# Taking the last two chunks of modes from their sums for the first two pairs of tiles

## The chip, the cores and the metric

The kernel runs on one core of one Trainium2 chip. The metric is the device time of one execution in microseconds (us), lower is better. A timed version is run several times beside the kernel before, on the same chip; the times quoted are medians unless a mean is named. A profile is one execution, so a number from a profile is one draw.

## The reference, cut to what matters

Causal attention of 8 batches x 8 heads x 576 positions feeds a spectral mixing layer:

```python
x = attn_out.transpose(0, 2, 1, 3).reshape(B, S, H * D)      # 8 x 576 x 512
X = np.fft.rfft(x, axis=1)
# 64 modes, each with its own complex 512 x 512 matrix:
Yr = einsum('bmd,mde->bme', Xr, w_r) - einsum('bmd,mde->bme', Xi, w_i)
Yi = einsum('bmd,mde->bme', Xr, w_i) + einsum('bmd,mde->bme', Xi, w_r)
y = np.fft.irfft(Y, n=S, axis=1)
u = x + y
out = u + np.maximum(u @ w_ch, 0.0)
```

The weights `w_r` and `w_i` are 2 x 64 x 512 x 512 f32. Reading them takes most of the time.

## The kernel before: the parts that matter

The 64 modes are taken in 8 chunks of 8. The inverse transform is a matmul with a constant matrix `G` (128 rows: mode, real or imaginary) and with `yv`, which holds y and v = y @ w_ch of all chunks by these 128 rows. A chunk's sums come out as rows of (mode, real or imaginary, batch), so a small transfer from on-chip memory to on-chip memory spreads them over `yv`:

```python
def spread(c, which, rows):
    nc.sync.dma_start(out=yv[16 * c : 16 * c + 16, :, which, :], in_=rows)

def modes(g, c, meanwhile=None):
    ps = auxpool.tile([P, DM], FP32, name="yp", tag="aux")
    for x in range(4):                       # x: one load of weights, 512 KB
        ...
        if x == 3 and meanwhile:
            meanwhile()                      # other matmuls ahead of the last load's
        for cg in range(4):
            nc.tensor.matmul(ps[32 * cg : 32 * cg + 32, :], ...)   # line 441
    ...
            spread(c, 0, yb)                 # last group: y of the chunk

def add_y(dst, i, which, rows=slice(0, P), start=False):   # line 674: from the spread rows
    ... nc.tensor.matmul(dst[x][r, :], G_sb[rows, ...], yv[rows, bb, which, :], ...)

def add_last(dst, i, yb, cols=slice(0, DM)):               # line 683: from a chunk's sums
    ... nc.tensor.matmul(dst[x][:, cols], Gx_sb[:, bass.ts(T, P)], yb[:, cols], ...)
```

`Gx_sb` is `G` of the last chunk, one row in eight, zeros between, so that it picks batch b out of a chunk's unspread sums. The results are made in 18 pairs of tiles. The first two pairs are started while the last weights arrive. The end of the stream of weights, where c is chunk 6 of 0 to 7:

```python
GK = P - 2 * MC                              # 112 rows: chunks 0 to 6
for i in range(NPRE):                        # NPRE = 2 pairs
    x_transposed(i)
x_times_wch(0, False)
yb = modes(NG - 1, c)
yt = y_transposed(yb, c)
y_times_wch(c, yt)                           # v of chunk 6, then spread(c, 1, vb)
x_times_wch(1, False)
start_u(0)
add_y(us[0], 0, 0, slice(0, GK))
def first_sums():
    for i in range(NPRE):
        add_y(z_of(i), i, 1, slice(0, GK))   # needs v of chunk 6 in yv
yb = modes(NG - 1, NCK - 1, first_sums)      # chunk 7
```

The softmax here doesn't subtract the row's maximum and nothing guards it: scores larger than these inputs give would overflow.

Of the kernel before, what the change touches and what calls it, by code (L numbers as in the profile page):

```python
# [9 lines left out]
FP32 = mybir.dt.float32  # L10
FP16 = mybir.dt.float16
# [7 lines left out]
def kernel(  # L19
# [11 lines left out]
    nc = tc.nc  # L31
    B, H, S, D = q.shape
    NM = moe_w_r.shape[0]
    DM = H * D
    P = 128
# [4 lines left out]
    NG = DM // P  # L40
# [5 lines left out]
    MC = 8  # L46
    NCK = NM // MC
# [3 lines left out]
    NF = NT - 1  # L51
# [10 lines left out]
        axis=1,  # L62
# [11 lines left out]
    G_np = np.zeros((NM, 2, SP), dtype=np.float64)  # L74
    G_np[:, 0, :S] = cmv[:, None] * np.cos(ang.T)
    G_np[:, 1, :S] = -(cmv[:, None] * np.sin(ang.T))
    G_np = G_np.reshape(P, SP).astype(np.float16)
# [6 lines left out]
    d_Ff = nc.inline_tensor(Ff_np, name="c_Ffwd").ap()  # L84
    d_G = nc.inline_tensor(G_np, name="c_Ginv").ap()

    Gx_np = np.zeros((2 * MC, B, NF * P), dtype=np.float16)
    Gx_np[:, 0] = G_np[-2 * MC :, : NF * P]
    d_Gx = nc.inline_tensor(Gx_np.reshape(P, NF * P), name="c_Ginvx").ap()

    ctx.enter_context(tc.manual_schedule())
    gp = ctx.enter_context(tc.tile_pool(name="globals", bufs=1))
# [98 lines left out]
    def ring_of(k):  # L191
        if k < NE:
            return None
        return int(k < LW2 and (k - NE) % (WA + WB) >= WA)
# [33 lines left out]
    for n in range(N):  # L228
# [3 lines left out]
        while nt < min(w, len(wq)):  # L232
            i = ring_of(nt)
# [37 lines left out]
    with tc.tile_pool(name="cum_psum", bufs=1, space=PSUM) as cpsum:  # L271
# [5 lines left out]
            out=cum, data0=spos, data1=zer, initial=0.0, op0=ALU.add, op1=ALU.add  # L277
# [16 lines left out]
        for x in range(2):  # L294
            rows = slice(NL * x, NL * x + NL)
            nc.vector.tensor_copy(
                out=cumt4[rows, :], in_=cumt_sb[rows, NK, x::2]
# [132 lines left out]
    def modes(g, c, meanwhile=None):  # L430


        ps = auxpool.tile([P, DM], FP32, name="yp", tag="aux")
        for x in range(4):
            ri, par = divmod(x, 2)
            cols = xs[g % 2].rearrange("p k r b m -> p (k r b) m")
            c0 = (48, 16)[ri] - 16 * par
            if x == 3 and meanwhile:
                meanwhile()
            for cg in range(4):  # L440
                nc.tensor.matmul(  # L441
                    ps[32 * cg : 32 * cg + 32, :],
                    cols[:, c0 : c0 + 32, c * MC + 2 * cg + par],
                    wt[(g, c, ri, par)][:, cg, :],
                    start=(x == 0), stop=(x == 3),
                    tile_position=(0, 32 * cg), skip_group_check=True,
                )
        if g == 0:
            nc.vector.tensor_copy(out=y_acc[:, c, :], in_=ps)
        elif g < NG - 1:  # L450
            nc.vector.tensor_tensor(out=y_acc[:, c, :], in0=ps, in1=y_acc[:, c, :], op=ALU.add)
        else:
            yb = spool.tile([P, DM], FP16, name="y_sb", tag="y")
            for cols in halves if c == NCK - 1 else [slice(0, DM)]:
                nc.vector.tensor_tensor(
                    out=yb[:, cols], in0=ps[:, cols], in1=y_acc[:, c, cols], op=ALU.add
                )
            spread(c, 0, yb)
            return yb
# [3 lines left out]
    def spread(c, which, rows):  # L463

        nc.sync.dma_start(out=yv[16 * c : 16 * c + 16, :, which, :], in_=rows)
# [7 lines left out]
    NPRE = 2  # L473
# [45 lines left out]
    with tc.tile_pool(name="sc_psum", bufs=2, space=PSUM) as scpool, \  # L519
# [7 lines left out]
        for n in range(N):  # L527
# [9 lines left out]
            i = first_pairs[n - N + len(first_pairs)] if n >= N - len(first_pairs) else None  # L537
# [19 lines left out]

    finpool = ctx.enter_context(tc.tile_pool(name="fin_sb", bufs=1))
    yv = finpool.tile([P, B, 2, DM], FP16, name="yv")
    Gx_sb = finpool.tile([P, NF * P], FP16, name="Gx_sb")  # L560
    nc.sync.dma_start(out=Gx_sb, in_=d_Gx)
    upool = ctx.enter_context(tc.tile_pool(name="u_psum", bufs=2, space=PSUM))
    zpool = ctx.enter_context(tc.tile_pool(name="z_psum", bufs=2, space=PSUM))

# [13 lines left out]
    def parts(b, T):  # L578

        if T < NF:  # L580
            return [(slice(0, P), b, ident16h)]
        return [(slice(NL * i, NL * i + NL), b + i, ident16h[:NL, :NL]) for i in range(2)]

    def x_transposed(i):
        xts[i] = xt_sb[len(xts) % 2]
        for x, (b, T) in enumerate(pairs[i]):
            ps = upool.tile([P, DT, P], FP32, name="xt_ps", tag="u")
            for rows, bb, ident in parts(b, T):
                for dt in range(DT):
                    nc.tensor.matmul(  # L590
                        ps[:, dt, rows], x_all[: rows.stop - rows.start, dt, bb, T, :],
                        ident, start=True, stop=True, skip_group_check=True,
                    )
            nc.vector.tensor_copy(out=xts[i][:, x], in_=ps)

    def x_times_wch(i, last):
        zs[i] = z = zpool.tile([P, 2, DM], FP32, name="z_ps", tag="z")
        for x in range(2):
            for dt in range(DT):
                nc.tensor.matmul(  # L600
                    z[:, x, :], xts[i][:, x, dt, :], wch_sb[:, dt, :],
                    start=(dt == 0), stop=(last and dt == DT - 1), skip_group_check=True,
                )
# [16 lines left out]
    def y_transposed(yb, c=NCK):  # L620
        ps = auxpool.tile([P, DT, P], FP16, name="yt_ps", tag="aux")
        for dt in range(DT):
            nc.tensor.transpose(ps[:, dt, :], yb[:, bass.ts(dt, P)], ident16h)
        yt = yt_first[:, :, c, :] if c < NY else spool.tile([P, DT, P], FP16, name="yt_sb", tag="yt")
        nc.scalar.copy(out=yt, in_=ps)
        return yt

    def y_times_wch(c, yt):
        vp = auxpool.tile([P, DM], FP32, name="v_ps", tag="aux")
        for dt in range(DT):  # L630
            nc.tensor.matmul(
                vp, yt[:, dt, :], wch_sb[:, dt, :], start=(dt == 0), stop=(dt == DT - 1)
            )
        vb = spool.tile([P, DM], FP16, name="v_sb", tag="v")
        nc.vector.tensor_copy(out=vb, in_=vp)
        spread(c, 1, vb)
        return vb
# [27 lines left out]
    order_z = list(late)  # L665
    TAKE = (3, 2, 2, 0, 2, 1)
    us, rs = {}, {}
    GK = P - 2 * MC

    def add_y(dst, i, which, rows=slice(0, P), start=False):  # L670

        for x, (b, T) in enumerate(pairs[i]):
            for r, bb, _ in parts(b, T):
                nc.tensor.matmul(  # L674
                    dst[x][r, :], G_sb[rows, bass.ds(T * P, r.stop - r.start)],
                    yv[rows, bb, which, :], start=start, stop=True, skip_group_check=True,
                    tile_position=(0, r.start),
                )

    def add_last(dst, i, yb, cols=slice(0, DM)):  # L680

        for x, (b, T) in enumerate(pairs[i]):
            nc.tensor.matmul(
                dst[x][:, cols], Gx_sb[:, bass.ts(T, P)], yb[:, cols],
                start=False, stop=True, skip_group_check=True,
            )

    def start_u(i):
        pool, tag = ((upool, "u"), (auxpool, "aux"))[i % 2]
        us[i] = [pool.tile([P, DM], FP32, name="u_ps", tag=tag) for x in range(2)]  # L690
        for x, (b, T) in enumerate(pairs[i]):
            for r, bb, ident in parts(b, T):
                nc.tensor.matmul(  # L693
                    us[i][x][r, :].rearrange("p (g d) -> p g d", d=P), ident,
                    x_all[: r.stop - r.start, :, bb, T, :],
                    start=True, stop=False, skip_group_check=True, tile_position=(0, r.start),
                )
# [35 lines left out]
    def z_of(i):  # L733
        return [zs[i][:, x, :] for x in range(2)]

    for c in range(NCK - 2):
        yb = modes(NG - 1, c)
        for x in range(TAKE[c] - 1):
            work()
        yt = y_transposed(yb, c)  # L740
        if TAKE[c]:
            work()
        if c >= NY:
            y_times_wch(c, yt)
        elif c == NY - 1:
            for b in range(B):
                first_times_wch(b)
    work()
    assert not order_z and not ahead
    c = NCK - 2  # L750
    for i in range(NPRE):
        x_transposed(i)
    x_times_wch(0, False)
    yb = modes(NG - 1, c)
    yt = y_transposed(yb, c)
    y_times_wch(c, yt)
    x_times_wch(1, False)


    start_u(0)  # L760
    add_y(us[0], 0, 0, slice(0, GK))

    def first_sums():
        for i in range(NPRE):
            add_y(z_of(i), i, 1, slice(0, GK))

    yb = modes(NG - 1, NCK - 1, first_sums)

    yt = spool.tile([P, DT, P], FP16, name="yt_sb", tag="yt")
    for x in range(2):  # L770
        dts = slice(x * DT // 2, (x + 1) * DT // 2)
        ps = auxpool.tile([P, DT // 2, P], FP16, name="yt_ps", tag="aux")
        for dt in range(dts.start, dts.stop):
            nc.tensor.transpose(ps[:, dt - dts.start, :], yb[:, bass.ts(dt, P)], ident16h)
        nc.scalar.copy(out=yt[:, dts], in_=ps)
    add_last(us[0], 0, yb)
    vb = spool.tile([P, DM], FP16, name="v_sb", tag="v")
    for cols in halves:
# [10 lines left out]
        relu(i, 2 - i)  # L789
    start_u(1)  # L790
    add_y(us[1], 1, 0, slice(0, GK))
    add_last(us[1], 1, yb)


# [65 lines left out]
```

## Time and profile before

| | before |
|---|---|
| three runs known ahead | 460.05, 460.65, 462.11 us |
| the profiled run | 460.51 us, span 458.7 us |
| stream of weights | until about 414 us, then a tail until 418.5 us |
| run of PE matmuls to the end | from about 424 us |

The page's totals of the engines and its row of the granted PE clock (40 slices of 11.5 us, in tenths of full clock) of the kernel before:

```profile
PE 349.6 (76%) x4201; PEld 219.9 (48%) x4201; DVE 236.8 (52%) x527; ACT 219.5 (48%) x382; POOL 182.9 (40%) x269
PEclk9998995999677979966779979799989778988999
```

No engine is near 100% over the span, but each stage has its own limit. The dips in the second line are slices of which a part was granted half clock.

### The profile page before, as it was taken

What the parts mean: (1) busy time and instruction counts of PE and PEld (TensorE: products, weight loads), DVE (VectorE), ACT (ScalarE), POOL (GpSimd) and SP (SyncE); (2) the same over time, 40 slices, a digit from 0 to 9 for tenths busy, and PEclk for the clock granted to TensorE, in tenths of its full rate; (3) what the DMA queues carried; (4) which work ended last, traced back from release to release, by engine and by line L of the source; (5) the groups of instructions that cost most, each with busy time, mean ns of one, the idle gap of its engine ahead of it and who ended that gap; (6) DMA issues with size and microseconds to landing.
All of it is one profiled execution on the core that took longest, in us unless ns stands there. A gap on an engine that the chain in (4) does not pass through costs nothing.

```text
span 458.7 us, 10278 instructions
## 1 busy us (share of the span) xinstructions
PE 349.6 (76%) x4201; PEld 219.9 (48%) x4201; DVE 236.8 (52%) x527; ACT 219.5 (48%) x382; POOL 182.9 (40%) x269
## 2 busy tenths in 40 slices
PE   1879979975663979948497677889977769778995
PEld 1456656753442656624365444556643336434442
DVE  7775654753332646623355444466556416441775
ACT  1586865564242746733356435456612220311895
POOL 6665555544345455344454444455232232100000
PEclk9998995999677979966779979799989778988999
DMA  9999999999999999999999999999999999994688
GB/s 177 201 202 203 201 201 204 202 204 204 205 203 200 202 203 203 204 205 204 198 196 204 204 204 203 204 203 203 205 208 213 210 210 210 214 216 79 237 282 319
DMA packets 109487, 94.63 MB, mean 206 GB/s; under 512 B 28480, under 2 KB 104640, under 8 KB 109440
## 3 DMA queue, kind: packets, MB, share of 16 engines
q0 software_dynamic: 98960, 81.81, 112.6%
q1 hardware_dynamic: 10480, 12.17, 8.5%
q8 instruction: 33, 0.54, 0.4%
q14 instruction: 14, 0.11, 0.1%
HBM read 164.66 MB, written 9.44 MB: 380 GB/s over the span
## 4 chain that ended last, share of the span: by engine, by line
DMA 66%; PE 22%; issue 4%; POOL 3%; DVE 2%; ACT 1%; DVEq 0%; POOLq 0%; ACTq 0%
DMA w_sb<-in_moe_w_i_dram 25%; DMA w_sb<-in_moe_w_r_dram 17%; DMA q<-in_q_dram 13%; DMA k<-in_k_dram 5%; PE sc_ps L365 3%; PE yp L441 3%; DMA x_all<-in_moe_w_r_dram 2%; PE sc_ps L359 2%; DMA y_acc<-in_moe_w_r_dram 2%; PE av_ps L394 2%; PE z_ps L674 2%; PE tr_ps L324 2%; DMA y_acc<-in_moe_w_i_dram 2%; PE u_ps L693 2%; PE u_ps L674 2%
## 5 line engine op out<-in xcount | busy, mean ns | idle before, releaser
L373 ACT ACTIVATE p_sb<-sc_ps,cumt_sb 128x576 f16<-128x576 f32 (+1 forms) x256 | 142.1, 636 | 49.3 <-PE sc_ps L365 48.8
L217 POOL DMA_DIRECT2D w_sb<-in_moe_w_i_dram x60 | 45.1, 751 | 81.6 <-PE yp L441 36.6
L217 POOL DMA_DIRECT2D w_sb<-in_moe_w_r_dram x60 | 45.4, 757 | 65.1 <-DMA w_sb<-in_moe_w_r_dram 28.2
L217 POOL DMA_DIRECT2D v<-in_v_dram x72 | 50.8, 708 | 33.1 <-DMA w_sb<-in_moe_w_r_dram 8.6
L359 PE MATMUL sc_ps<-negm,ident 128*128 128x256 bf16 x256 | 56.3, 306 | 0.2
L324 PE MATMUL tr_ps<-ident,q 64*64 64x64 bf16 x576 | 17.5, 210 | 49.2 <-DMA q<-in_q_dram 49.2
L441 PE MATMUL yp<-w_sb,xs 128*32 128x512 bf16 x480 | 38.0, 419 | 19.0 <-DMA w_sb<-in_moe_w_i_dram 14.7
L327 DVE COPY qtA<-tr_ps 64x576 bf16<-64x576 bf16 x32 | 23.7, 742 | 45.0 <-PE tr_ps L324 45.0
L394 PE MATMUL av_ps<-v,p_sb 128*128 128x65 f16 x1024 | 45.1, 199 | 0.0
L365 PE MATMUL sc_ps<-qtB,ktB 128*128 128x512 bf16 (+2 forms) x192 | 43.6, 344 | 0.0
L344 ACT ACTIVATE p<-sc_ps,cumt 128x64 f16<-128x64 f32 x32 | 10.1, 315 | 69.8 <-PE sc_ps L340 69.8
L394 PEld LDWEIGHTS <-p_sb 128*128 128x128 f16 x1024 | 40.1, 101 | 5.1 <-issue 1.2
L327 DVE COPY ktA<-tr_ps 64x576 bf16<-64x576 bf16 x32 | 24.0, 749 | 32.2 <-PE tr_ps L324 32.2
L324 PEld LDWEIGHTS <-q 64*64 64x64 bf16 x576 | 13.6, 123 | 51.8 <-DMA q<-in_q_dram 51.0
L365 PE MATMUL sc_ps<-qtA,ktA 65*128 65x512 bf16 (+2 forms) x192 | 37.9, 308 | 0.4 <-DMA qtA<-ncum_sb 0.4
L441 PEld LDWEIGHTS <-xs 128*32 128x32 bf16 x512 | 22.8, 170 | 29.8 <-issue 26.5
L399 DVE TENSOR_REDUCE den<-av_ps 128x5 f32<-128x10 f32 x64 | 10.8, 169 | 50.5 <-PE av_ps L394 50.5
L404 DVE TENSOR_TENSOR x_all<-av_ps,rcp 128x320 f16<-128x320 f32 x64 | 31.5, 492 | 2.2
L327 ACT COPY ktB<-tr_ps 64x576 bf16<-64x576 bf16 x32 | 20.3, 636 | 20.8 <-DVE ktA L327 19.9
L324 PE MATMUL tr_ps<-ident,k 64*64 64x64 bf16 x576 | 17.1, 208 | 15.9 <-DVE qtB L327 11.2
L365 PEld LDWEIGHTS <-ktB 128*128 128x128 bf16 x192 | 22.2, 116 | 14.5 <-issue 5.8
L600 PE MATMUL z_ps<-wch_sb,xs 128*128 128x512 f16 x96 | 26.2, 423 | 0.0
(111 smaller groups left out, 530.1 us busy)
## 6 DMA issues: line engine op xcount, KB each, us to landing
w_sb<-in_moe_w_r_dram POOLq DMA_DIRECT2D x60, 512.0 KB, 11.9
w_sb<-in_moe_w_i_dram POOLq DMA_DIRECT2D x60, 512.0 KB, 12.1
q<-in_q_dram POOLq DMA_DIRECT2D x32, 144.0 KB, 10.0
k<-in_k_dram POOLq DMA_DIRECT2D x32, 144.0 KB, 10.1
v<-in_v_dram POOLq DMA_DIRECT2D x72, 64.0 KB, 9.7
out_dram<-r_sb SPq DMA_DIRECT2D x16, 256.0 KB, 2.4
out_dram<-r_w SPq DMA_DIRECT2D x16, 256.0 KB, 2.6
x_all<-in_moe_w_i_dram POOLq DMA_DIRECT2D x3, 512.0 KB, 9.8
```

The costliest lines, as they stand in the source:

```text
L217: nc.gpsimd.dma_start(out=dst, in_=src)
L324: nc.tensor.transpose(ps[rows, r, :], src[rows, r, :], ident16[rows, rows])
L327: copy(out=dst[n % NQ][rows, :].rearrange("d (p r) -> d p r", r=R), in_=ps[rows].rearrange("d r p -> d p r"),)
L359: nc.tensor.matmul(ps[:, bass.ds(w * S, W)], ident16, negm[:, bass.ts(r, W)], start=True, stop=False, skip_group_check=True,)
L365: nc.tensor.matmul(ps[:, c0 : c0 + i1 - i0], keys[:, w, r, :], qt[:, i0:i1], start=False, stop=True, skip_group_check=True,)
L373: nc.scalar.activation(out=pt[:, poff[x] : poff[x] + S - w * W], in_=ps[:, w * S : (w + 1) * S - w * W], func=ACTF.Exp, bias=cumt_sb[:, x, ...
L394: nc.tensor.matmul(ps[:, I, r : r + NCH], lhsT, rhs, start=(i == 0), stop=(i == len(todo) - 1), skip_group_check=True,)
L399: nc.vector.tensor_reduce(out=den, in_=ps[:, :, 0 : VW : NCH], axis=mybir.AxisListType.X, op=ALU.add)
L404: nc.vector.tensor_tensor(out=x_all[:, g, b, :, D * h : D * h + D], in0=ps[:, :, 1 : NCH], in1=rcp.unsqueeze(2).to_broadcast([P, NT, D]), ...
L441: nc.tensor.matmul(ps[32 * cg : 32 * cg + 32, :], cols[:, c0 : c0 + 32, c * MC + 2 * cg + par], wt[(g, c, ri, par)][:, cg, :], start=(x == ...
L600: nc.tensor.matmul(z[:, x, :], xts[i][:, x, dt, :], wch_sb[:, dt, :], start=(dt == 0), stop=(last and dt == DT - 1), skip_group_check=True,)
L674: nc.tensor.matmul(dst[x][r, :], G_sb[rows, bass.ds(T * P, r.stop - r.start)], yv[rows, bb, which, :], start=start, stop=True, skip_group_ ...
```

## The change

Its intent: the z sums of the first two pairs should not wait for the copy of chunk 6's v into `yv`. Both last chunks are taken from their sums, with constants for two chunks. So that these don't double the transfer, only the 16 rows that are not zero are moved, into a cleared tile.

```diff
-    Gx_np = np.zeros((2 * MC, B, NF * P), dtype=np.float16)
-    Gx_np[:, 0] = G_np[-2 * MC :, : NF * P]
+    NX = 2
+    Gx_np = np.stack([G_np[2 * MC * c :, : NF * P][: 2 * MC] for c in range(NCK - NX, NCK)], axis=1)
 ...
-    Gx_sb = finpool.tile([P, NF * P], FP16, name="Gx_sb")
-    nc.sync.dma_start(out=Gx_sb, in_=d_Gx)
+    Gx_sb = finpool.tile([P, NX, NF * P], FP16, name="Gx_sb")
+    nc.vector.memset(Gx_sb.rearrange("p c t -> p (c t)").bitcast(FP32), 0.0)
+    nc.sync.dma_start(out=Gx_sb[0:P:B], in_=d_Gx)
 ...
-    GK = P - 2 * MC
+    GK = P - 2 * MC * NX
 ...
-    for i in range(NPRE):
-        x_transposed(i)
+    x_transposed(0)
     x_times_wch(0, False)
-    yb = modes(NG - 1, c)
-    yt = y_transposed(yb, c)
-    y_times_wch(c, yt)
+    yb6 = modes(NG - 1, c)
+    x_transposed(1)
+    yt = y_transposed(yb6)
     x_times_wch(1, False)
-    start_u(0)
-    add_y(us[0], 0, 0, slice(0, GK))
-    def first_sums():
+    vb6 = y_times_wch(c, yt)
+    def first_u():
+        start_u(0)
+        add_y(us[0], 0, 0, slice(0, GK))
+        add_last(us[0], 0, yb6, c=0)
+    def first_z():
         for i in range(NPRE):
             add_y(z_of(i), i, 1, slice(0, GK))
-    yb = modes(NG - 1, NCK - 1, first_sums)
+            add_last(z_of(i), i, vb6, c=0)
+    yb = modes(NG - 1, NCK - 1, {2: first_u, 3: first_z})
 ...
     add_y(us[1], 1, 0, slice(0, GK))
+    add_last(us[1], 1, yb6, c=0)
     add_last(us[1], 1, yb)
```

More of the change, by code (lines that the diff above doesn't have):

```diff
@@ L85 @@
     d_G = nc.inline_tensor(G_np, name="c_Ginv").ap()
-    Gx_np = np.zeros((2 * MC, B, NF * P), dtype=np.float16)
-    Gx_np[:, 0] = G_np[-2 * MC :, : NF * P]
-    d_Gx = nc.inline_tensor(Gx_np.reshape(P, NF * P), name="c_Ginvx").ap()
+    NX = 2
+    Gx_np = np.stack([G_np[2 * MC * c :, : NF * P][: 2 * MC] for c in range(NCK - NX, NCK)], axis=1)
+    d_Gx = nc.inline_tensor(np.ascontiguousarray(Gx_np), name="c_Ginvx").ap()
     ctx.enter_context(tc.manual_schedule())
@@ L437, in modes @@
             c0 = (48, 16)[ri] - 16 * par
-            if x == 3 and meanwhile:
-                meanwhile()
+            if meanwhile and x in meanwhile:
+                meanwhile[x]()
             for cg in range(4):
@@ L678, in add_y, with add_last @@
                 )
-    def add_last(dst, i, yb, cols=slice(0, DM)):
+    def add_last(dst, i, yb, cols=slice(0, DM), c=NX - 1):
         for x, (b, T) in enumerate(pairs[i]):
             nc.tensor.matmul(
-                dst[x][:, cols], Gx_sb[:, bass.ts(T, P)], yb[:, cols],
+                dst[x][:, cols], Gx_sb[:, c, bass.ts(T, P)], yb[:, cols],
                 start=False, stop=True, skip_group_check=True,
```

## The prediction

> **What bounds the kernel now.** I read the page first, then the chain of waits from 404 us on, then the timeline and the windows of that stretch, and last the landing of the last load of weights. The page gives the outline:
>
> ```profile
> DMA  9999999999999999999999999999999999994688
> DMA 66%; PE 22%; issue 4%; POOL 3%; DVE 2%; ACT 1%; DVEq 0%; POOLq 0%; ACTq 0%
> ```
>
> The first line is the busy share of the transfers in 40 slices of 11.5 us: full until slice 36, which ends near 413 us. The second is the chain that ended last: two thirds of it is DMA. So the kernel has two parts. Until about 414 us it streams weights. After 424 us it is a run of matmuls: in 424 to 454 us PE is busy 29.56 of 30.00 us (the windows view), and the chain there is PE alone. The change touches neither, only the joint between them, from 396 to 426 us. Its chain (columns: start us, us, what):
>
> ```profile
> 407.60 0.70 DVE y_sb L455
> ...
> 409.48 1.90 PE v_ps L631 x4
> 411.38 0.02 issue
> 411.40 0.70 DVE v_sb L635
> 412.10 0.02 issue
> 412.12 5.40 DMA yv<-v_sb
> 417.52 0.04 issue
> 417.56 1.02 PE z_ps L674 x4
> 418.58 0.43 PE yp L441 x4
> 419.02 0.02 issue
> 419.04 0.44 DVE y_sb L455
> ```
>
> This is chunk 6 of the modes (the last but one): its sum y, its product v, then a copy of 5.40 us that spreads v over the rows of `yv`, and only then the four z sums of the first two pairs, which read those rows. Behind them stand the last four matmuls of chunk 7. The change removes that 5.40 us wait, and it looks like the whole prize. The timeline tells what PE really lost to it:
>
> ```profile
> 417.56 1.02 PE L674 MATMUL z_ps<-yv,G_sb 112*128 112x512 f16 x4 [1.46 <-DMA yv<-v_sb]
> 418.53 0.46 PE L441 MATMUL yp<-w_sb,xs 128*32 128x512 bf16 x4
> ```
>
> PE idled 1.46 us, not 5.40; the rest of the copy lay beside work. And the matmuls behind it have a wait of their own. The issue of their weights, the last load of all, by its line:
>
> ```profile
> L217 POOL DMA_DIRECT2D w_sb<-in_moe_w_i_dram x1: 742/742/742, 396.6 to 396.6; - x1
> DMA to landing us min/median/max: 21.9/21.9/21.9
> ```
>
> Issued at 396.60 and landed 21.9 us later: 418.5. The four matmuls began at 418.53. So two waits end within 0.1 us of each other, and the chain can show only one. **The bound behind the one removed is the last load of weights, with almost no room in front of it.**
>
> **What the Trainium skill says.** (1) "DMA: Bandwidth & Descriptors", section "Queues, rings and completion order": each transfer engine takes turns, packet by packet, between the queues that have work for it. So a small copy shares time with the weights and delays them by about its own share. The trace agrees with the first half: the copies into `yv` issued at 397.3 to 412.1 took some 5.4 to 6.0 us to land, the last one, issued at 423.30 with the weights done, took 2.9 us. (2) "TensorE: Matmul & The Clock Gate", section "What's actually happening": the array runs at half clock after a window of some 3.4 us with too little work, at full clock after a busy one, and the windows run free of the program. The trace agrees:
>
> ```profile
> 409.40:412.80 3.40, 3.32 (x8) 1.16 (x9) 0.69 (x1) 0.02 (x1) 0.00 (x0) 0.50 1.23 214
> 412.80:416.20 3.40, 3.19 (x21) 1.28 (x20) 0.00 (x0) 0.00 (x0) 0.00 (x0) 0.99 1.00 185
> 416.20:419.60 3.40, 1.51 (x10) 0.55 (x9) 0.56 (x2) 0.00 (x0) 0.00 (x0) 1.00 0.25 49
> 419.60:423.00 3.40, 3.36 (x16) 2.04 (x17) 0.78 (x3) 0.75 (x2) 0.00 (x0) 0.51 0.13 39
> ```
>
> Each line is a stretch, its length, busy time of PE, PEld, DVE, ACT and POOL, then granted clock, DMA share and GB/s. PE is busy 1.51 of 3.40 us in the third, where it waits, and the fourth is granted 0.51. (3) "VectorE: DVE Perf Modes", section "Zero memsets can be issued as uint32 (trn2)": a memset costs one cycle per element whatever the type. The trace agrees: 576 elements take 538 ns as f32 and as bf16.
>
> **The change part by part.**
>
> *Constants.* The one transfer of 128 KB (128 rows x 512 x 2 bytes) becomes a memset of 128 x 512 f32 and a transfer of 16 rows x 1024 x 2 bytes = 32 KB. The memset is 512 x 538/576 = 0.48 us; in the old trace DVE is idle from about 341.2 to 343.11 us, waiting for PE, just where the instruction order puts it, so it costs nothing. The 96 KB saved were moved at 340 us in a full stream of about 205 GB/s: 96 x 1024 / 205,000 = 0.48 us that the weights behind get back. I take 0.4 us, as the packets of the two queues need not cost the same.
>
> *Order around chunk 6.* The transposes of pair 1 move behind the modes of chunk 6, into the hole where PE waited 0.80 us for y; the z product of pair 1 moves ahead of v. Chunk 6 itself waits for its own last weights at about 407.1 us, so starting it earlier gains nothing. v now comes after eight more matmuls (1.73 us warm, up to 3.4 us at half clock), so I put it at 413 to 414 us and its spread at about 414. Nobody needs that spread before pair 2, at 426 us. Coming later it also takes less from the end of the weights: an estimate of 0.2 us.
>
> *The sums.* Eight matmuls of 128x512 are added: two for u of pair 0 and four for z, before the last modes; two for u of pair 1, after them. In the PE chain of the last part two matmuls take 0.43 us. The z sums now need v from DVE at about 414, not its landed copy. Chunk 7's third load landed by about 415.6 us, as the four matmuls that read it stand at the end of a group that ran from 414.84 to 416.11. With it 0.4 us earlier: 415.2, plus 0.4 for its matmuls, plus eight sums at 0.215 = 1.7, and PE is through at about 417.3. The last weights land at 418.5 - 0.4 - 0.2 = 417.9. **PE waits for them, and not for the sums.** The last modes start at 417.9 in place of 418.53: 0.6 us won, of the 1.46 us that seemed on offer. The six sums ahead are free.
>
> *After the last modes.* (a) Two more matmuls for u of pair 1, +0.43 us, on the PE chain with nothing to hide them. (b) In 416.2 to 419.6 PE will be busy some 1.1 us with sums, 0.4 us with modes and then transposes and u sums, 2.2 to 2.6 of 3.4 us and not 1.51, so the next stretch may keep the full clock. There lie two u sums (0.85 us) and eight v products (1.72 us); at full clock they would take half, and with the waits for y and ACT between them I estimate up to 1.1 us saved. Since 1.92 of 3.40 us in 406.0 to 409.4 was followed by half clock, where the limit lies is open, and the windows' phase need not repeat; I count 0.5 us.
>
> Sum: -0.6 - 0.5 + 0.43 = about -0.7 us.
>
> **The rivals.** *The full wait comes back* (1.46 us, and the warm clock too): nothing else would hold PE until the last modes. That would make -1.46 - 1.1 + 0.43 = -2.1 us, 458.5. Against it stands the landing at 418.5; it needs the weights a whole microsecond earlier, and the stream was full up to 414.5 us. *The weights take the wait's place entirely*: the saved 96 KB and the later spread do not speed up their last packets, the clock goes cold as before, and only the two added matmuls remain: +0.4 us, 461.1. For it speaks that in 415 to 417.5 us the DMA share is only 0.5 to 0.76: some transfer engines have finished and the slowest decide. *PE becomes the bound*: if half clock falls on the sums, eight cost 3.4 us rather than 1.7, and the last modes start near 419; then +1 us, 461.7. Against it: at least 2.5 us of work in the window before, which in the old trace was enough for 0.99. *DMA of the last spread*: v of chunk 7, issued at 423.30, landed at 426.2, just as pair 2 asked for it (426.25); the two added matmuls give it 0.43 us more, so it does not bind.
>
> **Range and chances.** 460.65 - 0.7 gives 459.9 us. The three old runs lie between 460.05 and 462.11, so noise is as large as the effect; with the rivals at 458.5 to 461.7, I set 459.0 to 461.2. Two per cent is 9.2 us, while everything at stake in the joint is under 3 us: within 2% at 98 in 100, and one each for surprises.
>
> **What would show it.** In the changed trace: no PE wait for a copy into `yv` near 417; the last four modes waiting for `w_sb` instead, by a few tenths of a microsecond, and starting at 417.6 to 418.2; the last load landing about 21.3 us after its issue; eight more matmuls from `Gx_sb` rows; the clock near 1.0 in the stretch after the last modes if (b) is right. The prediction is wrong if the last weights land over 1 us earlier or later, if PE is still in the sums when they land, or if the memset delays the first y.

## The result, and the profile after

| | before | changed |
|---|---|---|
| median of 6 runs | 461.24 us | 459.02 us |
| lowest to highest | 460.05 to 462.53 | 458.77 to 459.84 |
| ratio of the means | | 0.9954, 95% interval 0.9932 to 0.9976 |
| span of the profiled run | 458.7 us | 457.1 us |

A ratio is the mean time of one kernel's fast runs over that of the other's of the same rounds, so it is not quite the ratio of the medians. The changed kernel is 0.46% faster: within 2%, clear of noise, and about 2.1 us rather than the 0.7 us forecast.

The changed kernel's chain of waits in the joint (start us, us, what):

```profile
396.06 22.01 DMA w_sb<-in_moe_w_i_dram
418.07 0.04 issue
418.11 0.48 PE yp L441 x4
418.58 0.03 issue
418.61 0.43 DVE y_sb L455
...
420.13 0.45 PE v_ps L785 x4
```

The copy of v is gone from the chain. In its place stands the last load of weights, landed at 418.07. The last modes follow 0.04 us later. In the timeline the eight products of v of chunk 7 now take 1.04 us, where they took 1.92. The timeline of the same stretch, the z sums and what stands before and after them:

```profile
416.83 0.60 PE L684 MATMUL z_ps<-v_sb,Gx_sb 128*128 128x512 f16 x2
...
418.11 0.45 PE L441 MATMUL yp<-w_sb,xs 128*32 128x512 bf16 x4 [0.68 <-DMA w_sb<-in_moe_w_i_dram]
```

PE was through with its sums near 417.4 and waited 0.68 us, now for weights. The windows view (length, busy PE, PEld, DVE, ACT, POOL, then granted clock, DMA share, GB/s) over the stretches that the prediction showed:

```profile
409.40:412.80 3.40, 3.40 (x22) 1.45 (x20) 0.86 (x2) 0.10 (x1) 0.00 (x0) 1.00 1.23 212
412.80:416.20 3.40, 2.23 (x14) 0.93 (x13) 0.00 (x0) 0.00 (x0) 0.00 (x0) 1.00 0.97 180
416.20:419.60 3.40, 2.15 (x15) 0.95 (x14) 0.76 (x2) 0.13 (x1) 0.00 (x0) 1.00 0.19 38
419.60:423.00 3.40, 3.26 (x24) 1.99 (x22) 1.28 (x3) 1.58 (x5) 0.00 (x0) 1.00 0.20 55
```

The clock is 1.00 throughout, where the kernel before had 0.50 in the first and 0.51 in the last of the four.

So the span is cut in two at the landing of the last weights. Before: 418.49 + 40.26 = 458.75. Changed: 418.07 + 38.99 = 457.06. Of the 1.69 us between the two profiles, 0.42 lie before the landing and 1.27 after it.

### The profile page after: what moved, and what is told of

The parts are those of the page before. It is cut to its first block, busy times and chain, and to the rows that moved or that the text cites. A ratio compares the mean times of both kernels' runs of the same rounds, so it can differ in the third digit from the quotient of the medians.

```text
span 457.1 us, 10262 instructions
## 1 busy us (share of the span) xinstructions
PE 339.1 (74%) x4177; PEld 217.2 (48%) x4209; DVE 237.3 (52%) x528; ACT 219.1 (48%) x382; POOL 182.9 (40%) x269
## 4 chain that ended last, share of the span: by engine, by line
DMA 70%; PE 20%; issue 4%; POOL 3%; DVE 2%; DVEq 0%; POOLq 0%
DMA w_sb<-in_moe_w_i_dram 44%; DMA q<-in_q_dram 13%; DMA w_sb<-in_moe_w_r_dram 5%; PE yp L441 3%; PE sc_ps L365 3%; PE av_ps L394 2%; DMA x_all<-in_moe_w_r_dram 2%; DMA k<-in_k_dram 2%; PE sc_ps L359 2%; DMA y_acc<-in_moe_w_i_dram 2%; PE tr_ps L324 2%; DMA y_acc<-in_moe_w_r_dram 2%; PE u_ps L694 2%; PE z_ps L675 2%; PE u_ps L675 2%
## 5 line engine op out<-in xcount | busy, mean ns | idle before, releaser
L359 PE MATMUL sc_ps<-negm,ident 128*128 128x256 bf16 x256 | 55.0, 300 | 0.3
L441 PE MATMUL yp<-w_sb,xs 128*32 128x512 bf16 x480 | 37.0, 408 | 22.2 <-DMA w_sb<-in_moe_w_i_dram 18.1
L394 PE MATMUL av_ps<-v,p_sb 128*128 128x65 f16 x1024 | 43.7, 196 | 0.0
L394 PEld LDWEIGHTS <-p_sb 128*128 128x128 f16 x1024 | 38.9, 99 | 4.8 <-issue 0.7
L365 PE MATMUL sc_ps<-qtB,ktB 128*128 128x64 bf16 (+2 forms) x160 | 34.8, 322 | 3.7 <-issue 2.4
L365 PE MATMUL sc_ps<-qtA,ktA 65*128 65x512 bf16 (+2 forms) x192 | 36.1, 297 | 0.3 <-DVE ktA L327 0.3
```

Source lines behind the costliest of these rows:

```text
L359: nc.tensor.matmul(ps[:, bass.ds(w * S, W)], ident16, negm[:, bass.ts(r, W)], start=True, stop=False, skip_group_check=True,)
L365: nc.tensor.matmul(ps[:, c0 : c0 + i1 - i0], keys[:, w, r, :], qt[:, i0:i1], start=False, stop=True, skip_group_check=True,)
L394: nc.tensor.matmul(ps[:, I, r : r + NCH], lhsT, rhs, start=(i == 0), stop=(i == len(todo) - 1), skip_group_check=True,)
L441: nc.tensor.matmul(ps[32 * cg : 32 * cg + 32, :], cols[:, c0 : c0 + 32, c * MC + 2 * cg + par], wt[(g, c, ri, par)][:, cg, :], start=(x == ...
```

## The experiments

**Theory A.** The wait for the copy was worth little by itself, as the weights landed at the same time. The gain is weights that land a little sooner, and above all a clock that stays full after the last modes, less two added matmuls. **Rivals.** R1: the removed wait itself is the gain. R2: the smaller constants are. R3: the new order around chunk 6 is. Times in the first four runs are against 11 runs of the kernel before, median 460.64.

### e1_constants: the small constants alone, in the kernel before

```diff
-    nc.sync.dma_start(out=Gx_sb, in_=d_Gx)             # 128 rows of 1 KB
+    nc.vector.memset(Gx_sb.bitcast(FP32), 0.0)
+    nc.sync.dma_start(out=Gx_sb[0:P:B], in_=d_Gx)      # 16 rows of 1 KB
```

> The kernel before with one part of the change alone: its constants as 16 rows of 1 KB into a cleared tile (16 KB moved in place of 128 KB). Theory A (the gain is earlier weights, a clock that stays warm after the last modes, and what is left of it after two added matmuls): the last load of weights lands about 0.4 us sooner after its issue chain, the last modes still wait for the z sums and these for the copy of v, which also lands about 0.4 us sooner: 0.3 to 0.5 us faster than before, and the stretch after the last modes is still granted about half clock. Rival R2 (the constants alone are the gain): about 2 us faster. Rival R1 (the removed wait alone is the gain): no difference.

Measured: 459.89 (458.47 to 460.26), ratio 0.9967 (0.9948 to 0.9986). What the constants do to the stream can be read off almost without noise (all five profiles with the old constants have 3533 to 3537 packets here): the packets of the weights' queue between 336 and 354 us, around the transfer of the constants (queue, packets, MB, share). The kernel before, then this one:

```profile
q0 software_dynamic: 3534, 3.51, 117.4%
```

```profile
q0 software_dynamic: 3616, 3.59, 120.2%
```

At 3534 / 18 = 196 packets per us, 82 packets more are 0.42 us. The changed kernel, which moves 32 KB of constants, has 3605: 71 more, 0.36 us. So that term is right. The clock did not mend: the last stretch took 40.08 us from the landing to the end, with about half clock in 416.2 to 423 us. As to the time, about 1.5 us were gained (0.6 to 2.4 by the interval), more than the 0.3 to 0.5 that A expected. The profile of this run, 458.3 us, accounts for 0.4 only. None of its six runs lies in the upper group of times that the kernel before has (see the last two runs below); against the lower seven of the 11 runs alone, mean 460.55, its mean of 459.64 is 0.9 us faster. What the rest is, chance or the timing of the joint, was not settled. R2 is not refuted by the times alone; the later runs bear on it.

### e3_old_order: the changed kernel with the order of before

```diff
-    x_transposed(0)
+    for i in range(NPRE):
+        x_transposed(i)
     x_times_wch(0, False)
     yb6 = modes(NG - 1, c)
-    x_transposed(1)
     yt = y_transposed(yb6)
-    x_times_wch(1, False)
     vb6 = y_times_wch(c, yt)
+    x_times_wch(1, False)
```

> The changed kernel with one part undone: around chunk 6 the order is again as before (both transposes ahead of its modes, its v product ahead of the z product of pair 1). Theory A: the last modes wait for their weights all the same, PE is busier than before in the 3.4 us ahead of them, so nearly all of the gain stays: within 0.5 us of the changed kernel, that is 1.6 to 2.3 us faster than before. Rival R3 (the order fills the holes and keeps the clock warm, and that is the gain): half or more of the gain goes, 1 us or less faster than before.

Measured: 458.95 (458.56 to 459.42), ratio 0.9952 (0.9934 to 0.9970). The whole gain stays. Profile: weights landed 418.76, last modes 418.80, 38.84 us to the end, full clock. R3 falls: the new order is not needed.

### e2_order: the new order alone, in the kernel before

```diff
-    for i in range(NPRE):
-        x_transposed(i)
+    x_transposed(0)
     x_times_wch(0, False)
     yb = modes(NG - 1, c)
+    x_transposed(1)
     yt = y_transposed(yb, c)
-    y_times_wch(c, yt)
     x_times_wch(1, False)
+    y_times_wch(c, yt)
```

> The kernel before with one part of the change alone: its order around chunk 6 (transposes of pair 1 behind the modes, z product of pair 1 ahead of v), the sums still from the spread rows. Theory A: v comes later by the eight matmuls, so its copy lands about 0.5 us later and the z sums and the last modes with it; with the holes ahead filled the clock may be warmer: between 0.5 us slower and 0.5 us faster than before. Rival R3 (the order is the gain): 1 us faster or more.

Measured in a second set, beside 11 runs of before with median 461.09: 462.37 (461.01 to 463.69), ratio 1.0013 (0.9986 to 1.0041): no gain. Its timeline shows the removed wait at its worst:

```profile
418.69 1.86 PE L674 MATMUL z_ps<-yv,G_sb 112*128 112x512 f16 x4 [1.87 <-DMA yv<-v_sb]
420.49 0.68 PE L441 MATMUL yp<-w_sb,xs 128*32 128x512 bf16 x4
```

The weights had landed at 419.19. The copy landed late, the four sums then ran at half clock (1.86 us where the old profile had 1.02), and the last modes started at 420.49, 1.30 us after their weights. So the wait can cost far more than the 0.04 us of the first profile.

### e5_fill: the wait kept, the clock kept warm

Six matmuls that compute u of pair 0 again are put into the wait, in the kernel before:

```diff
     def first_sums():
+        for again in range(2):
+            for x, (b, T) in enumerate(pairs[0]):
+                nc.tensor.matmul(us[0][x]..., ident16h, x_all[:, :, b, T, :], start=True, stop=False)
+        add_y(us[0], 0, 0, slice(0, GK))
         for i in range(NPRE):
```

> The kernel before, its wait for the copy of v kept, with six matmuls put into the 1.46 us of that wait that compute u of pair 0 once more (the result is the same). Theory A: the PE is busy 2.8 of 3.4 us in that window, so the next stretch is granted full clock, and the time falls by about 1.1 to 1.4 us though the wait stays and the last modes start no earlier. Rival R1 (the removed wait itself is the gain): no gain, or 0.1 to 0.3 us slower.

Measured: 460.15 (459.5 to 461.52), ratio 0.9982 (0.9962 to 1.0001). In the time that is 0.8 us, barely told from nothing. The profile, though, isolates the clock:

```profile
416.20:419.60 3.40, 3.16 (x21) 1.32 (x17) 0.00 (x0) 0.00 (x0) 0.00 (x0) 1.00 0.27 51
419.60:423.00 3.40, 2.72 (x21) 1.74 (x22) 1.61 (x4) 0.70 (x3) 0.00 (x0) 1.00 0.14 39
```

PE is busy 3.16 us in the third stretch in place of 1.51, and the fourth is granted full clock. The instructions after the last modes are those of the kernel before. From the landing to the end they take 38.66 us in place of 40.26: **the half clock cost 1.6 us.** The whole span is shorter by only 1.02 us (457.73 against 458.75), as its weights landed at 419.07, 0.58 us later than in the old profile. In the times, A's 1.1 to 1.4 us was missed. The profiled run is the fastest of the six, and what held the others back is not shown.

### e9_constants_fill: small constants and the fill together

The edits of e1_constants and e5_fill, both in the kernel before; the wait stays.

> The kernel before with two changes that leave its wait for the copy of v where it is: the small constants, and the six matmuls that fill that wait. Theory A (earlier weights and a warm clock are the gain): 1.0 to 1.8 us faster than before, so within 0.5 us of the changed kernel, or better by up to 0.4 us, as no matmul is added after the last modes. Rival R1 (the removed wait is the gain): 0.3 to 0.5 us faster than before, from the constants alone.

Measured in the second set: 459.91 (459.22 to 461.41), ratio 0.9966 (0.9939 to 0.9992), about 1.5 us faster than before (0.4 to 2.8 by the interval). A was right in the size; whether it comes within 0.5 us of the changed kernel was not tested, as that kernel did not run in this set. But the run also shows what filling cannot do. In its profile the weights landed at 418.49 and the last modes began at 419.49, a whole microsecond later. Its timeline tells why:

```profile
415.87 0.59 PE L674 MATMUL u_ps<-yv,G_sb 112*128 112x512 f16 x2 [1.99 <-DMA yv<-v_sb]
416.39 0.90 PE L440 MATMUL yp<-w_sb,xs 128*32 128x512 bf16 x12
...
418.54 1.02 PE L674 MATMUL z_ps<-yv,G_sb 112*128 112x512 f16 x4
```

PE had already waited 1.99 us for a copy ahead of the u sums of pair 0, which read the rows of chunk 6 too. (The line names the copy of v, but that landed only at 418.20; the copy of y landed at 415.74, and these sums read y.) Everything came later, and the fill pushed the z sums behind the landing. The change takes this wait away as well, as its u sums of pair 0 take chunk 6 from y itself.

### e4_u1_rows: two matmuls fewer after the last modes

```diff
     start_u(1)
-    add_y(us[1], 1, 0, slice(0, GK))
-    add_last(us[1], 1, yb6, c=0)
+    add_y(us[1], 1, 0, slice(0, P - 2 * MC))
     add_last(us[1], 1, yb)
```

> The changed kernel, but u of pair 1, which comes after the last modes, takes chunk 6 from the spread rows again (they have landed 8 us before): two matmuls of 128x512 fewer in the last part. Theory A: those two are on the PE chain with nothing to hide them: 0.43 us faster than the changed kernel, about 2.5 us faster than before. Rival (they lie beside the relus and additions of the last part): no difference to the changed kernel.

Measured: 458.81 (458.39 to 459.29), ratio 0.9949 (0.9932 to 0.9965). From the landing to the end it took 38.51 us. To compare it with the changed kernel on one chip, both were run again in a last set, beside 11 runs of before with median 460.51.

### a1_after_again and e10_u1_rows_again

> The changed kernel, unchanged, to be compared on one chip with the version that takes chunk 6 of u of pair 1 from the rows: 2.0 us faster than before, all times within 1.1 us, the last modes released by the weights and full clock after them in the profile.

> The changed kernel with u of pair 1 from the rows again, beside the changed kernel on the same chip: two matmuls of 128x512 fewer after the last modes, 0.43 us by the PE chain: 0.3 to 0.5 us faster than the changed kernel in the means, and 0.4 to 0.5 us shorter from the start of the last modes to the end of the span in the profile. Rival: no difference.

Measured: the changed kernel 458.86 (458.40 to 460.12), ratio 0.9966 (0.9948 to 0.9985); with u of pair 1 from the rows 458.74 (458.08 to 459.21), ratio 0.9961 (0.9945 to 0.9976). From landing to end: 38.84 and 38.50 us. With the earlier pair, 38.99 and 38.51, the two matmuls cost 0.34 to 0.48 us in the profiles, as worked out. In the times the means differ by 0.26 us, which these runs do not separate from noise. For the changed kernel itself the expectation was partly missed: it was about 1.6 us faster than before and not 2.0, and its times lie within 1.72 us and not 1.1. The version is the best tried, by a hair: chunk 6's y has long been in the rows when pair 1 wants it.

### e6_big_constants: the changed kernel with its constants moved whole

```diff
-    nc.vector.memset(Gx_sb.rearrange("p c t -> p (c t)").bitcast(FP32), 0.0)
-    nc.sync.dma_start(out=Gx_sb[0:P:B], in_=d_Gx)      # 16 rows of 2 KB
+    nc.sync.dma_start(out=Gx_sb, in_=d_Gx)             # 128 rows of 2 KB, zeros in them
```

> The changed kernel with its constants moved whole, zeros and all: 128 rows of 2 KB, 256 KB instead of 32 KB, no memset. By the two profiles the 96 KB saved gave the weights about 0.33 us; 224 KB more should then take 0.75 us from them, and as the last modes wait for the last weights all of it should show: 0.6 to 0.9 us slower than the changed kernel. Rival (the weights have slack before the last modes): under 0.2 us slower.

Measured: 459.59 (459.35 to 460.04), ratio 0.9957 (0.9931 to 0.9983). Against the changed kernel's 459.02 that is 0.57 us, but from another set, and by the ratios to before it is as good. The stream shows the cost without doubt, in the same window from 336 to 354 us:

```profile
q0 software_dynamic: 3474, 3.45, 115.4%
```

3605 - 3474 = 131 packets, 0.67 us. Weights landed at 418.88, last modes at 418.92, 38.83 us to the end. So the small constants are worth some 0.7 us against this simpler form of the change, and even without them the change keeps most of its gain. With this R2 falls as the main cause.

### e7_late_copies: the copies of chunk 6 behind the weights

```diff
-            spread(c, 0, yb)
+            if c != NCK - 2:
+                spread(c, 0, yb)
 ...
     yb = modes(NG - 1, NCK - 1, {2: first_u, 3: first_z})
+    spread(NCK - 2, 0, yb6)
+    spread(NCK - 2, 1, vb6)
```

(and the same condition on the copy of v.)

> The changed kernel, but the two copies of chunk 6 into the rows (128 KB each), which nobody reads before pair 2, are issued only after the last modes. Theory A: they no longer share the transfer engines with the end of the weights, so the last load lands sooner, by 256 KB at the rate that the constants showed (0.33 us for 96 KB) about 0.8 us, until PE's own sums (done near 417.4 us) bind: 0.5 to 0.8 us faster than the changed kernel, if the copies still land before pair 2 wants them at 424.8. Rival (small copies fill gaps of the engines that are done early and do not delay the slowest): no difference.

Measured: 459.26 (458.88 to 461.46), ratio 0.9956 (0.9929 to 0.9983): no gain over the changed kernel. One half of A held: the weights landed at 417.79, the earliest of all profiles, and 21.14 us after the issue of the last load, where the other thirteen profiles have 21.85 to 22.11. So the two copies had cost the last load some 0.7 to 1.0 us. The other half turned against it:

```profile
421.22 4.06 DMA yv<-v_sb
425.28 0.05 issue
425.33 0.60 PE z_ps L677 x2
```

The copy of chunk 7's v, which takes 2.9 us alone (issued at 421.50, landed by 424.4 in the changed kernel), now shares the engines with the two that were held back and takes 4.06; pair 2 waits for it. What was saved ahead was lost behind, with more: 40.26 us from landing to end.

### b1_before_again and b2_before_again: what the first profile did not show

The times of before fall in two groups: of its 11 runs in the first set, seven lie between 460.27 and 460.93 and four between 461.84 and 462.25. (In the second set it is six up to 461.09 and five from 461.86 to 463.53; the expectations below speak of these. In the third it is nine and two.) The changed kernel's 12 runs lie between 458.40 and 460.12. The profile of before was of the lower group.

> The kernel before, unchanged, for a second profile of it: its times fall into two groups, about 460.2 to 461.1 and 461.8 to 463.5, and the profile at hand is of the lower group (460.51), where the copy of v and the last weights land within 0.1 us of what they release. Theory B: the upper group are executions in which the copy of v lands later, at half clock ahead of it, so that the z sums start after 418.6 and the last modes after 419.5, while the weights have landed by 418.6; so the wait that the change removes costs more on average than the first profile shows. Rival: the weights themselves land over 1 us later in those executions. If this run is of the lower group it shows nothing on this.

> The same as the run before it, for a third profile: of the two, one should be of the upper group (5 of 11 executions are). Theory B: in the upper group z sums after 418.6, weights in time, last modes after 419.5. Rival: weights late.

Both fell in the upper group, at 463.57 and 462.51 us (single runs, so their state is called unknown; they are within 0.9% of the fastest of this kernel). The first one's timeline:

```profile
417.54 0.59 PE L674 MATMUL u_ps<-yv,G_sb 112*128 112x512 f16 x2 [1.74 <-DMA yv<-y_sb]
...
419.95 1.87 PE L674 MATMUL z_ps<-yv,G_sb 112*128 112x512 f16 x4 [0.98 <-DMA yv<-v_sb]
421.75 0.69 PE L441 MATMUL yp<-w_sb,xs 128*32 128x512 bf16 x4
```

Here PE waited for both copies of chunk 6, that of y as well, and the sums ran at half clock. Its clock, by the windows:

```profile
416.40:419.90 3.50, 1.43 (x14) 0.68 (x15) 0.00 (x0) 0.00 (x0) 0.00 (x0) 1.00 0.33 63
419.90:423.30 3.40, 2.82 (x11) 0.73 (x10) 0.76 (x2) 0.00 (x0) 0.00 (x0) 0.50 0.00 0
```

Theory B was half right. The z sums started at 419.95 and 418.89, the last modes at 421.75 and 420.68, as it said. But the weights were late too: landed at 420.24 and 419.43, so the rival had its part. The last modes began 1.51 and 1.25 us after their weights, and 41.56 and 41.31 us passed from landing to end. Why the weights come later in such executions is open. Their last load was already issued later, at 398.31 and 397.35 in place of 396.60, so most of the delay arose further up the stream; also, in the first of the two, one of the 16 shares of the last load landed 1.8 us after the other fifteen.

All cuts together, from the traces (us):

| run | weights landed | last modes start | landing to end | clock after |
|---|---|---|---|---|
| before, first profile | 418.49 | 418.53 | 40.26 | half |
| b1_before_again | 420.24 | 421.75 | 41.56 | half |
| b2_before_again | 419.43 | 420.68 | 41.31 | half |
| e2_order | 419.19 | 420.49 | 41.17 | half |
| e1_constants | 418.25 | 418.59 | 40.08 | half |
| e9_constants_fill | 418.49 | 419.49 | 39.74 | full |
| e5_fill | 419.07 | 419.11 | 38.66 | full |
| changed, two profiles | 418.07, 418.28 | 418.11, 418.32 | 38.99, 38.84 | full |
| e3_old_order | 418.76 | 418.80 | 38.84 | full |
| e6_big_constants | 418.88 | 418.92 | 38.83 | full |
| e4, e10 (u1 from rows) | 418.51, 417.82 | 418.55, 417.86 | 38.51, 38.50 | full |
| e7_late_copies | 417.79 | 417.83 | 40.26 | full, then a copy |

In every kernel that takes chunk 6 from its sums the last modes follow their weights by 0.04 us, at full clock. In those that read the rows they may follow by up to 1.5 us, and mostly at half clock.

The table also gives the cost of half clock without the landing. From the start of the last modes to the end, the five profiles at half clock took 39.74 to 40.22 us, and the four at full clock without the two added matmuls (e5, e9, e4, e10) 38.46 to 38.73: about 1.4 us between the means, a little less than the 1.6 of one pair.

As for R1, the wait beyond the weights was 0.04 us in one profile of before and 1.51 and 1.25 us in the other two. No run takes the wait away and leaves the clock cold, and taking it away is what keeps the clock full. So R1 as the only cause does not fit the profile of the fill (wait kept, clock mended, 1.6 us less behind the landing), but the wait's own share of the measured 2.1 us is not isolated.

## Why the prediction was right, point by point

**What binds behind the removed wait: right.** The last modes wait for the last weights, at 418.11 (foreseen: 417.6 to 418.2), with PE done near 417.4 (foreseen: 417.3).

**Two waits that end within 0.1 us: true of one execution.** The forecast took the copy's cost beyond the weights to be nothing. In two further executions of the same kernel it was 1.51 and 1.25 us. There PE also waited for the copy of chunk 6's y, 1.74 and 1.93 us, ahead of the u sums of pair 0: a second wait that the change removes and that the forecast did not list. The forecast knew the highest run, 462.11, but read the spread as noise around one state of the joint. This is one part of the difference between the 0.7 us forecast and the 2.1 us measured: without the three upper runs the mean of before is 460.34 and not 461.25, only 1.2 us above the changed kernel's 459.14. In the three later sets the upper group raises the mean of before by 0.4 to 1.0 us. How much of that is the wait and how much the late weights, two profiles do not settle: of the 3.05 and 1.99 us by which they exceed the first, 1.75 and 0.94 lie before the landing. The other part is the clock, below. The rival "the full wait comes back", set aside for the landing at 418.5, came nearest in size (2.1 us); its mechanism, weights a whole microsecond earlier, was not seen between the first profiles.

**Constants: right.** 0.4 us foreseen, 0.36 us by the count of packets. But the sign given for this and the next term was wrong: the last load did not land about 21.3 us after its issue, it took 22.01 us (21.89 before). The constants move at 340 us, so what they save must come ahead of that issue, which fell at 396.06 in place of 396.60. The memset took 0.485 us in an idle stretch of DVE, as worked out (0.48).

**A later copy helping the weights by 0.2 us: not seen.** v was foreseen at 413 to 414 us; with full clock ahead its copy was issued at 412.54, only 0.42 us later than before. The weights landed 0.42 us sooner, about what the constants explain, not 0.6. That agreement of two profiles is partly luck: with the same constants the weights landed anywhere from 417.82 to 418.76 in the changed kernel, e3, e4 and e10. That the copies do delay the last load is shown by e7; a shift of 0.42 us was too little to show.

**The clock: right in kind, mis-sized.** This is the term that failed: 0.5 us counted, up to 1.1 estimated. The fill shows 1.6 us for the same instructions (40.26 against 38.66). Most of it lies where it was put: from the first transpose of chunk 7's y to the start of the last z sums the chain takes 3.80 us before (419.52 to 423.32) and 2.44 us with the fill (420.10 to 422.54), 1.36 less. The forecast had half of 0.85 + 1.72 us, 1.29, cut it to 1.1 for waits in between that did not eat it, and then halved it for doubt whether the clock would hold. It held in every profile of the changed kernel and its variants, seven in all.

**Two added matmuls: right.** 0.43 us foreseen, 0.34 to 0.48 in the profiles.

Summed again with measured terms, for the two first profiles: -0.42 - 1.6 + 0.4 = -1.6 us, and the spans differ by 1.69. The forecast's terms were -0.6 - 0.5 + 0.43, so the clock is off by 1.1 us and the landing by 0.2 the other way. The means differ by 2.1 us, and there the upper group of before counts as well.

The time of 459.02 lies inside the range by 0.02 us, which is luck: the mechanism was right, but the size of the clock term and the upper group were not foreseen. What stays open: the wait's own share, how much of the gain of e1_constants in time is chance, and why the stream itself ends later in the upper group.

## What to carry to other kernels

When two waits end together in a profile, the chain names one of them: look up the other's landing before counting on the removal of the first, and take a second profile before calling either of them free. A short idle of PE ahead of a PE-bound stretch can cost twice, once as idle and once as half clock behind it, and work moved into the hole can mend the second. Here the half clock cost 1.6 us in a profile in which the idle itself cost nothing. A small copy was not free beside a full stream (0.7 to 1.0 us for the two copies of chunk 6), and moving it behind the stream cost about 1.3 us there.

## What the Trainium skill lacked or had wrong

- "TensorE: Matmul & The Clock Gate", section "What's actually happening", says that half clock follows an idle window of 3.4 us, but not how idle. Over the 1,380 such windows at full clock in the fourteen traces, cut at the clock's own steps, none with PE busy more than 2.21 us was followed by half clock, and every one with less than 1.75 us was, but for two at the very end of a run (1.44 us in e3_old_order, 1.47 in a1_after_again). In between both are seen. So PE can be busy for over half of a window and still be slowed.
- "DMA: Bandwidth & Descriptors" gives round-robin between queues but no time for a small copy beside a full one. Here 128 KB between two places on the chip took 5.4 to 6.5 us beside the weights, 2.9 us alone, and 4.06 us behind three of its kind.
- The same page, section "Latency and other measured facts", names two engines as usually slower. In the first profile of before the 16 shares of the last load landed in two groups of eight, by 415.46 and from 416.22 to 418.49 us: half of the shares were late, by up to 3 us. The trace does not tell which engines carried them.
